# Later blocks' layer normalisation one slot later and behind VectorE's earlier work; V's split two slots behind its squares

## The chip, the cores and the metric

The kernel runs on one core of a Trainium2 chip. TensorE (PE) multiplies matrices, VectorE (DVE), ScalarE (ACT) and GpSimd (POOL) do the elementwise work, and SyncE (SP) mostly issues transfers. Each engine has an order of its own, fixed when the kernel is built; between engines, semaphores hold an instruction until its data are there. The metric is the device time of one execution, in microseconds; lower is better.

## The reference

Three parts run one behind the other on a batch of 4 sequences of 576 rows of 512: block-causal attention with 8 heads, a feed-forward network with layer normalisation and a residual, and a second one in front of which the rows are mixed by a two-dimensional Fourier transform.

```
# attention: q, k, v (4, 8, 576, 64), mask by blocks of 64
scores = scale * np.matmul(q, k.transpose(0, 1, 3, 2))
scores = np.where(mask, scores, -1000000000.0)
attn = np.exp(scores - np.max(scores, axis=-1, keepdims=True))
attn = attn / (np.sum(attn, axis=-1, keepdims=True) + 1e-09)
x = np.matmul(attn, v)                    # then heads side by side: (4, 576, 512)
# first feed-forward network
xn = (x - mu) / np.sqrt(var + 1e-06) * g_ln
x = x + np.maximum(xn @ w_ch1, 0.0) @ w_ch2       # 512 -> 2048 -> 512
# mixing and second feed-forward network
u = x + np.real(np.fft.fft(np.fft.fft(x, axis=1), axis=2))
un = (u - mu) / np.sqrt(var + 1e-06)
return u + np.maximum(un @ w_ch1_2, 0.0) @ w_ch2_2
```

## The kernel before

Every float32 operand of a large product is split into two fp16 parts (high and low), and three products of the parts take the place of one.

**Tiles.** The 2304 rows lie in nine blocks of 256, two half blocks of 128 each (`t` = 0, 1): E0 to E3 and F0 to F3, two for each sequence, and L, which collects 32 + 32 rows of each sequence. Attention works in units of a sequence and a pair of heads; each unit has three steps `j` = 2, 3, 4, which produce N, and when the last unit of a sequence is through, `a_x` moves N by GpSimd's DMA queue into XxF and XxL. E blocks are ready early, so the first network runs in the order E0 E1 E2 E3 F0 F1 L F2 F3 beside the attention of later sequences.

**One block of the first network.** `ln` computes mean and variance (bn_stats, bn_aggr) and, in twelve small operations (L532 to L547), one over the root. For each half block `ln_hi` normalises (xn, L564) and takes the high part (xs, ScalarE L571), `ln_lo` the low part (xs, VectorE L594) and issues a transposing transfer to xnT on SP (L595). There is one buffer each of xn, xs and xnT. Then come eight groups of products with the first weights (G1, `gemm1`, L627), each with two operations that make hT (L636, L637), and the products with the second weights (G2, `gemm2`, L652), half block by half block; the result is added to the rows of X (L664).

**Attention.** Scores (L1143, L1152), their maximum (aq, L1163, L1164), exponential (L1167), fp16 parts P (L918, L919), transposing transfers to PT on SP (L925), products with V (pv, L890), the division by the row sum (rr, L932, L935) and N (L1212, L1218). V is split into vh and vl: `a_norm` takes its squares, `a_total` sums them over partitions on GpSimd, `a_split` makes a power of two from it (pw, four operations, L835 to L842) and the two parts (L1127, L1128).

**Second weights.** From some 430 us on the second network's weights are decoded: a load wr (L202), a sign (ScalarE L217), ws (VectorE L218), squares (junk, L239), their sum (wn, wt), a scale (wsc, again four operations from L835 on), wq (L331, L339) and a spill to memory d (L348). The mixing of the rows (pq, ya, y) begins behind it.

**What sets the order.** Each part is a stream of items with a due time. `merge` takes the stream whose time is least, but not before the items that it needs are there (`have`), and so writes one program. A scheduler then orders each engine's instructions; within limits it moves one forward if its operands are there by its own estimate. `tc.issue_after(i)` is an edge that keeps what is written under it behind instruction `i`. In attention's stream `at(t, rank, f, u)` puts step `f` of unit `u` into slot `t`; a slot is 4.0 long, `f = 3 * n` is the slot in which unit `n` starts, P_N = 4, P_D = 0. `gives` says which slot makes a block's rows available to the first network.

Of the kernel before, what the change touches and what calls it, by code (L numbers as in the profile page):

```python
# [8 lines left out]
F32 = mybir.dt.float32  # L9
# [8 lines left out]
B, H, S, D = 4, 8, 576, 64  # L18
# [25 lines left out]
P_D = 0  # L44
# [34 lines left out]
P_N = 4  # L79
P_R = 0.5  # L80
# [19 lines left out]
def fused_kernel(ctx: ExitStack, tc: tile.TileContext, io: dict):  # L100
    nc = tc.nc
# [5 lines left out]
    sm = ctx.enter_context(tc.tile_pool(name="sm", bufs=2))  # L107
# [415 lines left out]
    def ln(ffn, c):  # L523
        x = X[c]
        w = sm.tile([128, 20], F32, tag="ln", bufs=2, name=f"ln{ffn}{c}")
        mv = w[:, 0:4].rearrange("p (t k) -> p t k", t=2)
        for t in range(2):
            st = sm.tile([128, 6], F32, tag="bn", bufs=2, name=f"bn{ffn}{c}{t}")
            nc.vector.bn_stats(out=st, in_=x[:, t, :])
            nc.vector.bn_aggr(out=mv[:, t, :], in_=st)  # L530
        v, e, y, a, y2 = (w[:, i:i + 2] for i in (4, 6, 8, 10, 12))
        nc.vector.tensor_scalar(  # L532
            out=v, in0=mv[:, :, 1], scalar1=1e-6, scalar2=None, op0=ALU.add
        )
        nc.vector.tensor_scalar(
            out=e.bitcast(I32), in0=v.bitcast(I32), scalar1=-1, scalar2=1,
            op0=ALU.bitwise_xor, op1=ALU.logical_shift_right,
        )
        nc.vector.tensor_scalar(
            out=y, in0=e, scalar1=float(0.677 * 2.0 ** -65), scalar2=None, op0=ALU.mult  # L540
        )
        for it in range(3):
            nc.vector.scalar_tensor_tensor(
                out=a, in0=y, scalar=-0.5, in1=y, op0=ALU.mult, op1=ALU.mult
            )
            nc.vector.tensor_tensor(out=a, in0=a, in1=v, op=ALU.mult)
            nc.vector.scalar_tensor_tensor(  # L547
                out=y2, in0=a, scalar=1.5, in1=y, op0=ALU.add, op1=ALU.mult
            )
            y, y2 = y2, y  # L550
        if (ffn, c) == (1, ("E", 0)):
            xnT[ffn, c] = a_tile([128, 2, 4, 256], F16, "xnT0", "xnT0")
        else:
            xnT[ffn, c] = fpool.tile([128, 2, 4, 256], F16, tag="xnT", bufs=1, name=f"xnT{ffn}{c}")
        lnst[ffn, c] = (mv, y)

    def ln_hi(ffn, c, t):
        mv, y = lnst[ffn, c]
        own = (ffn, c) in TURN
        if own:  # L560
            xn = a_tile([128, DM], F32, "xn0", "xn0")
        else:
            xn = fpool.tile([128, DM], F32, tag="xn", bufs=1, name="xn")
        nc.vector.tensor_scalar(  # L564
            out=xn, in0=X[c][:, t, :], scalar1=mv[:, t, 0:1], scalar2=y[:, t:t + 1],
            op0=ALU.subtract, op1=ALU.mult,
        )
        if own:
            return ln_turn(ffn, c, t, xn)
        xs = fpool.tile([128, 2, DM], F16, tag="xs", bufs=1, name="xs")  # L570
        nc.scalar.activation(out=xs[:, 0, :], in_=xn, func=AF.Copy)  # L571
        lnst[ffn, c, t] = (xn, xs)
# [16 lines left out]
    def ln_lo(ffn, c, t):  # L589
        if (ffn, c) in TURN:  # L590
            return
        xn, xs = lnst.pop((ffn, c, t))
        eng = nc.gpsimd if (ffn, t) in LNP else nc.vector
        eng.tensor_tensor(out=xs[:, 1, :], in0=xn, in1=xs[:, 0, :], op=ALU.subtract)  # L594
        nc.sync.dma_start_transpose(  # L595
            out=xnT[ffn, c].rearrange("p a k t -> p (a k) t")[:, :, t * 128:(t + 1) * 128],
            in_=xs.rearrange("p a f -> p (a f)"),
        )

    def ln_steps(ffn, c):  # L600
        return [
            (0.0, lambda: ln(ffn, c)), (0.0, lambda: ln_hi(ffn, c, 0)),
            (0.0, lambda: (ln_lo(ffn, c, 0), ln_hi(ffn, c, 1))), (0.0, lambda: ln_lo(ffn, c, 1)),
        ]

    def run(steps):
        for _, f in steps:
            f()
# [212 lines left out]
    def a_tile(shape, dt, tag, name):  # L821
        return ap_["p"].tile(shape, dt, tag=tag, bufs=ap_["b"][tag], name=name)
# [418 lines left out]
    def attention_items(order):  # L1241
        units = [(u, j) for u in order for j in (2, 3, 4)]
        ev = {}

        def at(t, rank, fn, *a):
            ev.setdefault(t, []).append((rank, len(ev.get(t, [])), fn, a))

        for n, u in enumerate(order):
            f = 3 * n
            at(max(f - 3 - L_N, f - 6), 9, a_load, u)  # L1250
            at(f - P_N, P_R, a_norm, u)
            at(f - P_N + P_D, P_R, a_total, u)
            at(f - P_N + P_D, P_R, a_split, u)
        lag = (0,) + LG
        gives = {}
        for t, (u, j) in enumerate(units):
            at(t, RK[0], a_s, u, j)
            at(t + lag[1], RK[1], a_exp, u, j)
            at(t + lag[2], RK[2], a_norm_p, u, j)
            at(t + lag[3], RK[3], a_pv, u, j)  # L1260
            at(t + lag[4], RK[4], a_evac, u, j)
            if j == 4 and u[1] == NPAIR - 1:
                at(t + lag[5], RK[5], a_x, u[0])
                gives[t + lag[5]] = ("X1", ("F", u[0]))

        def emit(t):
            for rank, n, fn, a in sorted(ev.get(t, []), key=lambda x: x[:2]):
                if fn is a_s and "f" in ff_last:
                    with tc.issue_after(ff_last["f"]):
                        fn(*a)  # L1270
                else:
                    fn(*a)

        return [
            (4.0, lambda t=t: emit(t), (), gives.get(t)) for t in range(min(ev), max(ev) + 1)
        ]
# [251 lines left out]
    if True:  # L1528
# [41 lines left out]
        AE = [e_items(b) for b in range(B)]  # L1570
        A1 = [(0.0, a_switch, (("W", 1, 2, 3), ("X1", ("E", 3))), None)]
        A1 += attention_items([(b, p) for b in range(B) for p in range(NPAIR)])
        A1 += [(0.0, a_end, (), ("X1", "L"))]

        LN = []

        def ffn_items(ffn, order, both=(), mixed=None):
            seq = []
            for n, c in enumerate(order):
                x = ("X", ffn, c) if ffn == 2 else ("X1", c)  # L1580
                behind = ((("G1",) + TURN[0] + (5,)),) if (ffn, c) == TURN[1] else ()
                lns = [(0.0, f, (x,) + behind, None) for _, f in ln_steps(ffn, c)]
                g1_needs = ()
                if ffn == 1 and n < LNA:
# [195 lines left out]
```

## Time and profile before

| | us |
|---|---|
| three runs | 994.78, 996.1, 999.83; median 996.1 |
| profiled execution | 997.26 |
| its span | 995.5 |
| busy in the span: TensorE | 946.1 (95%) |
| VectorE | 673.7 (68%) |
| ScalarE | 490.2 (49%) |
| GpSimd | 72.5 (7%) |

The span is the time from the first to the last instruction in the trace; 1.8 us of the profiled execution lie around it. All times of the trace count from the start of the span. A wait is put down to the instruction that released it last: "pv <- DVE aq" says that TensorE's product pv could start when VectorE's aq was through, and that may be late because of something else in front of it on VectorE.

### The profile page before, as it was taken

To read this page: it belongs to the slowest core of one execution; us is meant where nothing else is said; L and a number is where in the kernel's file an instruction comes from. 1 tells how busy PE (TensorE), PEld (TensorE's weight loads), DVE (VectorE), ACT (ScalarE), POOL (GpSimd) and SP (SyncE) were. 2 spreads that over 40 slices of the span, in tenths; PEclk is the share of its full clock that TensorE was granted. 3 is DMA by queue.
4 is the path that set the end of the run, shared out by engine and by line. 5 is a ranking of instruction groups with operands and counts; after the bars stand their busy time and mean duration, and the time that the engine had idled before them with its cause. 6 is when DMAs were issued, how large, how long until landed. Compare 5 with 4: busy or idle time off the path is not lost.

```text
span 995.5 us, 19447 instructions
## 1 busy us (share of the span) xinstructions
PE 946.1 (95%) x7758; PEld 700.8 (70%) x7758; DVE 673.7 (68%) x1677; ACT 490.2 (49%) x852; POOL 72.5 (7%) x184
## 2 busy tenths in 40 slices
PE   8898989998998999998999889999999999999998
PEld 6786654674674674766576665858588888888887
DVE  3886696665767666566587887669476776765754
ACT  5887664554554564426656654325153352342431
POOL 1000000002001010040011120100000000000000
PEclk9998999999999999999999989999999999999999
DMA  7657536758667666567408657011110111101100
GB/s 259 225 186 212 133 79 138 153 114 154 139 126 154 129 146 103 99 139 298 146 8 249 212 177 255 8 22 65 43 22 23 33 23 33 22 23 43 23 22 22
DMA packets 159195, 110.95 MB, mean 111 GB/s; under 512 B 134141, under 2 KB 141318, under 8 KB 157056
## 3 DMA queue, kind: packets, MB, share of 16 engines
q1 hardware_dynamic: 154640, 104.87, 40.8%
q0 software_dynamic: 2352, 4.32, 1.9%
q8 instruction: 61, 1.00, 0.4%
q10 hardware_dynamic: 2112, 0.52, 0.2%
q14 instruction: 30, 0.25, 0.1%
HBM read 64.19 MB, written 11.01 MB: 76 GB/s over the span
## 4 chain that ended last, share of the span: by engine, by line
PE 42%; DVE 7%; DMA 5%; ACT 3%; issue 1%; POOL 0%; ACTq 0%; POOLq 0%; DVEq 0%; SPq 0%
PE g L698 15%; PE s L748 13%; PE g L627 6%; PE g L679 4%; PE g L652 3%; DMA wr<-in_w 2%; DMA xnT1L<-xs 1%; ACT junk L239 1%; DVE ws L218 1%; DVE wq L339 1%; ACT sign L217 1%; DVE hT L637 1%; PE ya L1433 1%; DMA xnT2('F', 0)_7977<-xs 1%; DMA d<-ws 1%
## 5 line engine op out<-in xcount | busy, mean ns | idle before, releaser
L627 PEld LDWEIGHTS <-wq 128*128 128x128 f16 x2112 | 206.5, 99 | 47.9 <-issue 19.0
L652 PE MATMUL g<-wq,hT 128*128 128x512 f16 x768 | 184.2, 383 | 2.1 <-ACT hT L636 1.3
L698 PEld LDWEIGHTS <-wq 128*128 128x128 f16 x1344 | 131.5, 98 | 15.4
L652 PEld LDWEIGHTS <-hT 128*128 128x128 f16 x768 | 74.6, 99 | 90.2 <-issue 5.8
L748 PEld LDWEIGHTS <-hs 128*128 128x128 f16 x1176 | 115.1, 98 | 13.3
L715 ACT ACTIVATE hr<-g,tk 128x256 f32<-128x256 f32 x112 | 47.0, 470 | 143.1 <-PE g L698 143.1
L890 PE MATMUL pv<-vh,PT 128*128 128x65 f16 (+1 forms) x704 | 102.9, 203 | 14.6 <-DMA PT<-P 5.3
L919 DVE SCALAR_TENSOR_TENSOR P<-e,P 128x768 f16<-128x768 f32 (+2 forms) x56 | 54.6, 976 | 69.9 <-ACT P L918 69.8
L890 PEld LDWEIGHTS <-PT 128*128 128x128 f16 x1056 | 82.1, 101 | 28.1 <-issue 19.0
L723 DVE TENSOR_TENSOR hr<-hr 128x128 f32<-128x128 f32 x224 | 65.4, 292 | 48.3 <-ACT hr L715 40.4
L1167 ACT ACTIVATE e<-st,aq 128x384 f32<-128x384 f32 (+2 forms) x80 | 48.9, 652 | 91.3 <-DVE aq L1164 80.8
L748 PE MATMUL s<-tT,hs 128*128 128x256 f16 x672 | 75.7, 273 | 0.0
L637 DVE SCALAR_TENSOR_TENSOR hT<-g,hT 128x512 f16<-128x512 f32 x88 | 59.8, 683 | 19.3 <-ACT hT L636 19.1
L636 ACT ACTIVATE hT<-g 128x512 f16<-128x512 f32 x88 | 51.4, 588 | 34.2 <-PE g L627 34.1
L679 PE MATMUL g<-wq,hT 128*128 128x512 f16 x288 | 63.8, 379 | 0.2 <-DVE wq L339 0.2
L890 PE MATMUL pv<-vl,PT 128*128 128x64 f16 (+1 forms) x352 | 62.7, 203 | 0.0
L730 DVE TENSOR_TENSOR hs<-hr,hs 128x896 f16<-128x896 f32 x56 | 60.8, 1085 | 0.5
L748 PE MATMUL s<-tB,hs 128*128 128x256 f16 x504 | 57.3, 273 | 0.0
L218 DVE SCALAR_TENSOR_TENSOR ws<-wr,sign 128x512 int32<-128x512 int32 (+1 forms) x48 | 41.2, 863 | 23.2 <-ACT sign L217 20.6
L217 ACT ACTIVATE sign<-wr 128x512 f16<-128x512 bf16 (+1 forms) x48 | 46.5, 971 | 19.7 <-DMA wr<-in_w 19.0
L729 ACT ACTIVATE hs<-hr 128x896 f16<-128x896 f32 x56 | 53.1, 948 | 1.6 <-DVE hr L723 1.6
L679 PEld LDWEIGHTS <-hT 128*128 128x128 f16 x288 | 28.0, 98 | 32.4 <-issue 0.5
(425 smaller groups left out, 1516.4 us busy)
## 6 DMA issues: line engine op xcount, KB each, us to landing
wr<-in_w SPq DMA_DIRECT2D x16, 1023.5 KB, 6.0
wr<-in_w SPq DMA_DIRECT2D x32, 511.8 KB, 5.1
rawv<-in_vt SPq DMA_DIRECT2D x16, 320.0 KB, 2.9
k<-in_kt SPq DMA_DIRECT2D x16, 288.0 KB, 3.5
d<-ws SPq DMA_DIRECT2D x4, 1024.0 KB, 5.2
ws<-d SPq DMA_DIRECT2D x4, 1024.0 KB, 5.5
wt<-d SPq DMA_DIRECT2D x4, 1024.0 KB, 4.8
qz<-in_qt SPq DMA_DIRECT2D x32, 80.0 KB, 3.2
```

The source lines that it names most:

```text
L217: nc.scalar.activation(out=z[:, :, :, 1], in_=r.bitcast(BF16)[:, :, :, 2], func=AF.Copy)
L627: nc.tensor.matmul(out=ps[:, i, :], lhsT=w1(ffn, k, wh, m), rhs=xt[:, xh, k, :], start=(n == 0), stop=(n == 3 * KT - 1),)
L637: nc.vector.scalar_tensor_tensor(out=h[:, :, 1, :], in0=ps, scalar=0.0, in1=h[:, :, 0, :], op0=ALU.max, op1=ALU.subtract,)
L652: nc.tensor.matmul(out=ps, lhsT=h[f // 4][:, f % 4, hh, t * 128:(t + 1) * 128], rhs=w2(ffn, f, wh), start=(f == 0 and hh == 0 and wh == 0) ...
L679: nc.tensor.matmul(out=g2["b"][t], lhsT=h[f // 4][:, f % 4, hh, t * 128:(t + 1) * 128], rhs=w2(ffn, f, wh), start=(f == 0 and hh == 0 and ...
L698: nc.tensor.matmul(out=ps[:, q, :], lhsT=w1(2, k, wh, i + 8 * q), rhs=xt[:, xh, k, :], start=(n == 0), stop=(n == 3 * KT - 1),)
L723: done = nc.vector.tensor_tensor(out=r[:, o], in0=r[:, a], in1=r[:, b], op=op)
L729: nc.scalar.activation(out=h[:, 0], in_=r[:, 1:8], func=AF.Copy)
L730: nc.vector.tensor_tensor(out=h[:, 1], in0=r[:, 1:8], in1=h[:, 0], op=ALU.subtract)
L748: nc.tensor.matmul(out=ps, lhsT=h[:, hh, hb], rhs=T[nm][:, wh, i], start=(i == 0 and hh == 0 and wh == 0), stop=(i == 7 and hh == 1),)
L890: nc.tensor.matmul(out=out[..., 0:w], lhsT=l, rhs=v[..., 0:w], start=(n == 0), stop=(n == len(mm) - 1))
L919: nc.vector.scalar_tensor_tensor(out=P[:, 1, 0:n], in0=e, scalar=PSC, in1=P[:, 0, 0:n], op0=ALU.mult, op1=ALU.subtract)
```

## The change

There are three edits. In `ln`, for the blocks F0 to F3 and L of the first network, the statistics get an edge: they stay behind the last VectorE instruction that was written until then (`last_on`, new). In `attention_items`, `a_split` goes into slot f - 2; it was in f - 4, with `a_norm` and `a_total`. And the rows of F0, F1 and F2 (not those of the last sequence, F3) are given to the first network one slot later.

```diff
--- before.py
+++ after.py
@@ -524,10 +524,13 @@
         x = X[c]
         w = sm.tile([128, 20], F32, tag="ln", bufs=2, name=f"ln{ffn}{c}")
         mv = w[:, 0:4].rearrange("p (t k) -> p t k", t=2)
-        for t in range(2):
-            st = sm.tile([128, 6], F32, tag="bn", bufs=2, name=f"bn{ffn}{c}{t}")
-            nc.vector.bn_stats(out=st, in_=x[:, t, :])
-            nc.vector.bn_aggr(out=mv[:, t, :], in_=st)
+        with ExitStack() as order:
+            if ffn == 1 and c[0] != "E":
+                order.enter_context(tc.issue_after(last_on(mybir.EngineType.DVE)))
+            for t in range(2):
+                st = sm.tile([128, 6], F32, tag="bn", bufs=2, name=f"bn{ffn}{c}{t}")
+                nc.vector.bn_stats(out=st, in_=x[:, t, :])
+                nc.vector.bn_aggr(out=mv[:, t, :], in_=st)
         v, e, y, a, y2 = (w[:, i:i + 2] for i in (4, 6, 8, 10, 12))
         nc.vector.tensor_scalar(
             out=v, in0=mv[:, :, 1], scalar1=1e-6, scalar2=None, op0=ALU.add
@@ -602,6 +605,9 @@
             (0.0, lambda: ln(ffn, c)), (0.0, lambda: ln_hi(ffn, c, 0)),
             (0.0, lambda: (ln_lo(ffn, c, 0), ln_hi(ffn, c, 1))), (0.0, lambda: ln_lo(ffn, c, 1)),
         ]
+
+    def last_on(engine):
+        return next(i for i in reversed(nc.cur_bb.bb.instructions) if i.engine == engine)
 
     def run(steps):
         for _, f in steps:
@@ -1250,7 +1256,7 @@
             at(max(f - 3 - L_N, f - 6), 9, a_load, u)
             at(f - P_N, P_R, a_norm, u)
             at(f - P_N + P_D, P_R, a_total, u)
-            at(f - P_N + P_D, P_R, a_split, u)
+            at(f - P_N + 2, P_R, a_split, u)
         lag = (0,) + LG
         gives = {}
         for t, (u, j) in enumerate(units):
@@ -1261,7 +1267,7 @@
             at(t + lag[4], RK[4], a_evac, u, j)
             if j == 4 and u[1] == NPAIR - 1:
                 at(t + lag[5], RK[5], a_x, u[0])
-                gives[t + lag[5]] = ("X1", ("F", u[0]))
+                gives[t + lag[5] + (0 if u[0] == B - 1 else 1)] = ("X1", ("F", u[0]))
 
         def emit(t):
             for rank, n, fn, a in sorted(ev.get(t, []), key=lambda x: x[:2]):
```

The following pieces show what that does to the order of the engines. Line numbers of the changed kernel are 3 to 6 higher (L529 is L532, L594 is L597, L664 is L670, L919 is L925).

VectorE at F0's statistics, before: they stand in front of attention's P, maximum aq and N of a unit, behind nothing but the maximum (L1163, L1164) of the step before.

```order
L1164 TENSOR_SCALAR aq<-aq 128x2
L529 BN_STATS bn1('F', 0)0_3913<-XxF_2949 128x6
L529 BN_STATS bn1('F', 0)1_3916<-XxF_2949 128x6
L664 SCALAR_TENSOR_TENSOR XxE_1058<-g_2690,winv_1540,XxE_1058 128x512
L919 SCALAR_TENSOR_TENSOR P<-e,P 128x768
L1163 TENSOR_REDUCE aq<-st 128x2
L932 TENSOR_SCALAR rr<-pv,pw 128x2
L1164 TENSOR_SCALAR aq<-aq 128x2
L530 BN_AGGR ln1('F', 0)_3912<-bn1('F', 0)0_3913 128x2
L935 RECIPROCAL rr<-rr 128x2
L530 BN_AGGR ln1('F', 0)_3912<-bn1('F', 0)1_3916 128x2
```

The changed kernel, the same engine, some hundred rows later in its order, behind the first half of E3's output (XxE_1444):

```order
L670 SCALAR_TENSOR_TENSOR XxE_1444<-g_3656,winv_1540,XxE_1444 128x512
L925 SCALAR_TENSOR_TENSOR P<-e,P 128x1024
L938 TENSOR_SCALAR rr<-pv,pw 128x2
L1169 TENSOR_REDUCE aq<-st 128x1
L941 RECIPROCAL rr<-rr 128x2
L1170 TENSOR_SCALAR aq<-aq 128x1
L532 BN_STATS bn1('F', 0)0_3906<-XxF_2942 128x6
L1218 TENSOR_TENSOR N_3832<-pv,rr 128x128
L533 BN_AGGR ln1('F', 0)_3905<-bn1('F', 0)0_3906 128x2
L532 BN_STATS bn1('F', 0)1_3909<-XxF_2942 128x6
L925 SCALAR_TENSOR_TENSOR P<-e,P 128x576
```

F0's statistics moved behind attention's work of about three units, into the gaps between single rows of it.

VectorE at L's statistics, before: they stand between the hT of F1's G1 (L637) and the last N of attention, and F2's first statistics are among them.

```order
L637 SCALAR_TENSOR_TENSOR hT<-g_5213,hT 128x2x256
L637 SCALAR_TENSOR_TENSOR hT<-g_5270,hT 128x2x256
L529 BN_STATS bn1L_5543<-XxL 128x6
L530 BN_AGGR ln1L<-bn1L_5543 128x2
L529 BN_STATS bn1L_5546<-XxL 128x6
L529 BN_STATS bn1('F', 2)0_6040<-XxF_4756 128x6
L530 BN_AGGR ln1L<-bn1L_5546 128x2
L637 SCALAR_TENSOR_TENSOR hT<-g_5297,hT 128x2x256
L932 TENSOR_SCALAR rr<-pv,pw 128x2
```

The changed kernel: the hT of F1 come first, then ws, the second network's weights (L218), then the first half of F1's output (L670), then L's statistics.

```order
L643 SCALAR_TENSOR_TENSOR hT<-g_5402,hT 128x2x256
L218 SCALAR_TENSOR_TENSOR ws_5806<-wr_5804,sign_5490 128x512
L218 SCALAR_TENSOR_TENSOR ws_5806<-wr_5839,sign_5491 128x512
L218 SCALAR_TENSOR_TENSOR ws_5806<-wr_5845,sign_5490 128x512
L218 SCALAR_TENSOR_TENSOR ws_5806<-wr_5864,sign_5491 128x512
L670 SCALAR_TENSOR_TENSOR XxF_3846<-g_5429,winv_1540,XxF_3846 128x512
L532 BN_STATS bn1L_5543<-XxL 128x6
L532 BN_STATS bn1L_5546<-XxL 128x6
L533 BN_AGGR ln1L<-bn1L_5543 128x2
L250 TENSOR_REDUCE wn_5870<-wn 128x1
L533 BN_AGGR ln1L<-bn1L_5546 128x2
```

L's statistics moved behind four ws and XxF; F2's and F3's, which stood right behind them, went further back still.

SP's queue at L's transposes, before: the first stands behind attention's last PT, two weight loads lie between the two.

```order
L925 DMA_TRANSPOSE PT<-P 128x16x128
L925 DMA_TRANSPOSE PT<-P 128x10x128
L595 DMA_TRANSPOSE xnT1L<-xs 128x8x128
L202 DMA wr_5804<-in_w_2 128x2047
L202 DMA wr_5839<-in_w_2 128x2047
L595 DMA_TRANSPOSE xnT1L<-xs 128x8x128
L202 DMA wr_5845<-in_w_2 128x2047
L202 DMA wr_5864<-in_w_2 128x2047
L202 DMA wr_5875<-in_w_2 128x2047
```

The changed kernel: eight weight loads stand further up, and these rows follow.

```order
L202 DMA wr_5917<-in_w_2 128x2047
L202 DMA wr_5935<-in_w_2 128x2047
L202 DMA wr_5946<-in_w_2 128x2047
L202 DMA wr_5969<-in_w_2 128x2047
L348 DMA d_5897<-wq_5874 128x4096
L598 DMA_TRANSPOSE xnT1L<-xs 128x8x128
L202 DMA wr_5988<-in_w_2 128x2047
L202 DMA wr_5994<-in_w_2 128x2047
L598 DMA_TRANSPOSE xnT1L<-xs 128x8x128
```

L's transposes moved behind ten weight loads and the first spill (L348).

VectorE at F3's splits, before: both low parts (L594) stand in front of L's output (XxL, L664) of the first network.

```order
L218 SCALAR_TENSOR_TENSOR ws_6020<-wr_6234,sign_5491 128x512
L637 SCALAR_TENSOR_TENSOR hT<-g_5812,hT 128x2x256
L594 TENSOR_TENSOR xs<-xn,xs 128x512
L564 TENSOR_SCALAR xn<-XxF_5442,ln1('F', 3)_6702 128x512
L594 TENSOR_TENSOR xs<-xn,xs 128x512
L564 TENSOR_SCALAR xn<-XxF_5442,ln1('F', 3)_6702 128x512
L664 SCALAR_TENSOR_TENSOR XxL<-g_5851,winv_1540,XxL 128x512
L664 SCALAR_TENSOR_TENSOR XxL<-g_6005,winv_1540,XxL 128x512
```

The changed kernel, at F3's second low part (L597): the second half of F2's output (XxF_4749, L670) stands in front of it.

```order
L549 TENSOR_TENSOR ln2('F', 0)_7958<-ln2('F', 0)_7958 128x2
L550 SCALAR_TENSOR_TENSOR ln2('F', 0)_7958<-ln2('F', 0)_7958 128x2
L218 SCALAR_TENSOR_TENSOR ws_6764<-wr_7007,sign_5491 128x512
L670 SCALAR_TENSOR_TENSOR XxF_4749<-g_6689,winv_1540,XxF_4749 128x512
L597 TENSOR_TENSOR xs<-xn,xs 128x512
L250 TENSOR_REDUCE wn_7013<-wn 128x1
L1398 TENSOR_TENSOR xe<-XxE_1058,XxF_4749 128x1024
L841 TENSOR_SCALAR pw<-wt 128x1
```

F3's second split moved from in front of L's output to behind the end of F2's.

## Rows read from the trace of the kernel before

**Rows 1.** The page's table of busy time: engine, us busy, share of the span, instructions.
```profile
PE 946.1 (95%) x7758; PEld 700.8 (70%) x7758; DVE 673.7 (68%) x1677; ACT 490.2 (49%) x852; POOL 72.5 (7%) x184
```

**Rows 2.** Waits of TensorE, 170 to 560 us: engine, line, waited for: us, times, longest.
```profile
PE pv L890 <- DVE aq L1164: 4.0, 1, 4.0
PE g L627 <- DVE pw L842: 3.8, 2, 2.1
PE g L627 <- DVE hT L637: 3.5, 3, 2.0
PE g L627 <- DMA wr<-in_w: 2.6, 1, 2.6
PE pv L890 <- DVE N L1212: 2.5, 3, 1.6
PE pv L890 <- DVE ln1('F', 0)_3912 L532: 2.5, 1, 2.5
PE pv L890 <- DMA PT<-P: 1.5, 1, 1.5
```

**Rows 3.** Timeline of VectorE at F0: start, us, operation, xcount [idle before <-releaser].
```profile
244.72 0.69 DVE L529 BATCH_NORM_STATS2 bn1('F', 0)0_3913<-XxF 128x6 f32<-128x512 f32 x1 [4.51 <-DMA XxF<-N]
...
249.24 0.16 DVE L532 TENSOR_SCALAR ln1('F', 0)_3912<-ln1('F', 0)_3912 128x2 f32<-128x2 f32 x1
```

**Rows 4.** Windows behind two pauses: busy us by engine, then PEclk, DMA share, GB/s.
```profile
250.00:254.00 4.00, 4.00 (x19) 2.03 (x18) 3.72 (x14) 1.28 (x2) 0.20 (x1) 0.57 0.54 131
318.00:322.00 4.00, 4.00 (x20) 1.99 (x18) 3.17 (x8) 2.44 (x4) 0.00 (x0) 0.57 0.01 4
```

**Rows 5.** Timeline of VectorE at F1.
```profile
314.90 0.55 DVE L564 TENSOR_SCALAR xn<-XxF,ln1('F', 1)_4868 128x512 f32<-128x512 f32 x1
...
317.28 0.28 DVE L1212 TENSOR_TENSOR N<-pv,rr 128x128 f32<-128x128 f32 x1
```

**Rows 6.** Instructions on L's transposed rows xnT1L, waits, and time from issue to landing.
```profile
L627 PE MATMUL g<-xnT1L,wq x192: 269/273/421, 456.1 to 480.8; 128*128 128x256 f16 x192
...
  DVE hT L637: 2.0, 1
...
  ACT xs L571: 8.9, 1
...
DMA to landing us min/median/max: 3.1/7.9/12.6
```

**Rows 7.** Timeline of VectorE before L's matmuls.
```profile
451.26 0.69 DVE L594 TENSOR_TENSOR xs<-xn,xs 128x512 f16<-128x512 f32 x1 [8.88 <-ACT xs L571]
...
454.68 0.69 DVE L218 SCALAR_TENSOR_TENSOR ws<-wr,sign 128x512 int32<-128x512 int32 x1 [1.45 <-ACT sign L217]
455.29 0.74 DVE L664 SCALAR_TENSOR_TENSOR XxF<-g,winv,XxF 128x512 f32<-128x512 f32 x1
```

**Rows 8.** Lines L652 (425 to 460) and L627 (545 to 600): ns min/median/max, first and last start.
```profile
L652 PE MATMUL g<-wq,hT x96: 376/379/379, 432.6 to 453.1; 128*128 128x512 f16 x96
...
L627 PE MATMUL g<-xnT1('F', 3)_6721,wq x192: 270/273/421, 553.5 to 592.9; 128*128 128x256 f16 x192
```

**Rows 9.** Groups of VectorE by line, 425 to 560 us: busy us, mean ns.
```profile
L339 DVE SCALAR_TENSOR_TENSOR wq<-ws,wsc,wq 128x512 f16<-128x512 f32 x16 | 11.0, 744 | 1.8 <-ACT wq L331 1.8
```

**Rows 10.** Chain of waits, 540 to 600 us: start, us, what.
```profile
555.95 0.80 ACT sign L217
...
557.49 0.72 ACT junk L239 x2
...
577.75 1.25 PE pq L1467 x5
```

**Rows 11.** Waits of TensorE, 540 to 600 us.
```profile
PE pq L1467 <- ACT y L1440: 5.2, 2, 4.7
PE ya L1433 <- DVE y L1441: 1.9, 1, 1.9
```

**Rows 12.** Timeline of SP's queue at the spills.
```profile
559.64 0.33 SPq L348 DMA_DIRECT2D d<-ws  x1
```

## The prediction

> **What bounds the kernel now.** I read the page first: TensorE is busy 95% of the span, so an order of work can win time only where it stands still or runs at the low clock [rows 1]. Then the waits of TensorE in the stretch where the change acts (170 to 560 us, attention and the first feed-forward network): the seven longest entries make 20.4 us, 16.3 of them put down to VectorE [rows 2]. That is all a better order of VectorE could win there, plus the slow clock behind each pause. Last I read VectorE's timeline at those pauses, the windows of the clock, and the stretch around 577 us, where TensorE waits for the chain that decodes the second network's weights and prepares the mixing [rows 10, 11]. From 577.75 us on the chain of waits is TensorE alone [rows 10], so a gain or loss before it counts only if it gets past that point.
>
> The profiled execution took 997.26 us, 1.1 us above the median of the runs; the sum is made against it.
>
> **Attention stretch, normalisation of F0 and F1.** Before, F0's statistics are hoisted so far up that VectorE, which works in order, has nothing else from 240.2 us on and stands 4.51 us for the transfer of F0's rows, and the chain's small operations (0.16 us each) lie in front of attention's P and N [rows 3]. TensorE pays 2.5 us right behind it (the wait named L532) and, just before, 1.5 us for a PT that comes from a late P [rows 2]. F1's chain has its first normalisation at 314.90, the N behind it comes at 317.28, and TensorE stands 4.0 us for the aq behind that [rows 2, 5]. Now both chains stand some hundred rows of VectorE's order later (F0) and behind what was given (F1), mixed singly with attention's rows, and their transfers have landed. Gross: 2.5 + 1.5 + 4.0 = 8.0. Behind each of the two long pauses stands a stretch of 4 us at a granted clock of 0.57, that is mostly at the level of 1.2 GHz [rows 4]: 4 x 0.43 = 1.7 us each, 3.4 in all. Together 11.4 us.
>
> Against it: the same operations remain (four statistics of 0.69, two chains of twelve at 0.16, and per half block a normalisation of 0.55 and a split of 0.69 us [rows 3, 5, 7]) and still stand in front of some P or N. No row shows them there; bounds: nothing, or the pauses they made before, 11.4. I take the nearest rows, the three short waits for N (2.5 us together [rows 2]) and half as much again for the clock, about 4.0. Term: -7.4, between -11.4 and 0. The transposes of F0 and F1 land later but, by the order, still in front of the matmuls that read them; cover lost would cost one landing, 3.1 us [rows 6].
>
> **V's scale and split.** Two slots later in the stream, but VectorE's rows are the same up to F0, pw and vl included: the scheduler put them there anyway. The two waits for pw (3.8 us together [rows 2]) stay. Term 0; if slots further on do move, between -3.8 and +3.8.
>
> **The last block (L).** Before, its statistics were hoisted into attention's tail, its first transposes landed in 3.1 us, the second in 12.6, and its matmuls started at 456.1 [rows 6]. Now its statistics stand behind four ws and behind XxF's first half. The fourth ws was at 454.68 [rows 7]. It can come earlier, since before VectorE stood 8.88 us for ScalarE, which in its turn waited 8.9 us for the landing of 12.6 [rows 6, 7]; that wait is no longer in front of it. So the fourth ws lies between 445.8 and 454.7. From its start: ws 0.69, XxF 0.74, two statistics 1.38, two aggregates and twelve small ones 2.3, with four wq of 0.74 (3.0) [rows 9], six small operations on the weights' scale (1.0) and one normalisation (0.55) between: 9.6 us. ScalarE's first split 0.63, then four pairs of junk and sign in front of its second split, 4 x (0.72 + 0.80) = 6.1 [rows 10], 0.63, VectorE's 0.69, the landing 3.1: 11.2. L's matmuls so begin between 466.6 and 475.5, 10.5 to 19.4 us later; there is no other work for TensorE, whose last product of F1's G2 starts at 453.1 and lasts 0.4 [rows 8]. Ten weight loads and a spill stand in front of the first transposes now, so I do not take the early end but 468: +12. The wait of 2.0 us for hT inside L's matmuls [rows 6] goes, since ScalarE and VectorE are through with more of the decode by then: +10. The low clock behind the new pause I set at 1.7 us against as much that no longer follows the wait for hT: 0; no row shows what a pause of 12 us costs there.
>
> **F3.** Before, its splits were done with no wait for them. Now its second split stands on VectorE behind the second half of F2's output, which ends with G2 of F2. TensorE has nothing else then: 0.74 + 0.69 + 3.1 = 4.5, with issue some 4.7 us of pause, follows TensorE wherever it is. Upper bound: ScalarE's split waits behind a sign that was at 555.95 and the transposes behind the spill that was issued at 559.64 [rows 10, 12]; 559.64 + 0.33 + 3.1 = 563.1 against a start of 553.5 [rows 8], +9.6. F2's normalisation is late too, but still in front of its matmuls by the order: 0.
>
> **Sum.** TensorE reaches the mixing at -7.4 + 10 + 4.7 = +7.3. There it waited 1.9 + 5.2 = 7.1 us for y [rows 11]. If y keeps its time, these waits take up 7.1, and +0.2 is left. I let y keep it: VectorE wins up to 8.9 us of standing before and gets F3's 6.3 us of normalisation (1.38 + 2.3 + 1.1 + 1.4) into the stretch. 997.26 + 0.2 = 997.5; against the median of the runs, 1.1 lower, 996.4. I say 997.
>
> **Rivals.**
> *Slower: the transposes queue behind the weight loads.* L's second transposes took 12.6 us to land when loads were in flight, the first 3.1 [rows 6]. If both of L's, and F3's, land in 12.6, L's matmuls begin 9.5 us later than taken and F3's pause is 14.2 instead of 4.7: TensorE reaches the mixing at -7.4 + 19.5 + 14.2 = +26.3 at worst, past the 7.1 by 19; with only L's or only F3's, by about 10. I price it at 1007. It decides from the point where L's and F3's delays exceed 14.5 us together (7.4 + 7.1). For it: ten loads and two spills stand around these transposes now. Against: the wide landings of before fell on a stretch that also loads the mixing's constants. The rule behind it: the Trainium skill ("DMA: Bandwidth & Descriptors", Queues, rings and completion order) says that each DMA engine takes descriptors in ring order, and that SP owns one ring on each of them, so its loads and transposes share it; by it a transpose behind two loads waits for them, which favours this rival. The trace agrees for the second transposes of L, not for the first.
> *Faster: y comes earlier too.* If the decode, freed of the 8.88 us, carries y forward and L's delay is at its low end (+10.5 - 2 = +8.5), TensorE is at -7.4 + 8.5 + 4.7 = +5.8 and the pause of 7.1 is not all needed; with attention's term at its end (-11.4) it is at +1.8, and y up to 6 us earlier ends the time at 991; with y no limit at all, 990. For it: attention's waits are plain in the trace. Against: L and F3.
> *Nothing moves.* Were the waits put down to VectorE's chains really others', attention's term would be 0, and so would a good deal of the rest, 997. The order does change, so this is small.
>
> **How the numbers follow.** Forecast (losses in the tail take up the gain, 992 to 1003) 0.42; slower rival 0.30; faster rival 0.22; nothing moves 0.06. About 0.5%, 5 us, is what a measurement of this kernel can tell from no change: 991 to 1001. Faster: the rival's 0.22 and 0.04 of the forecast's low side, 0.26. Slower: 0.30 and 0.06 of its high side, 0.36. Same: 0.38. The range, 986 to 1010, takes in the ends of the rivals but for some 0.1 on each side.
>
> **What would show it.** Right: no wait of 4.0 and 2.45 us for VectorE between 240 and 320 us; the waits for pw still there; a pause of 10 to 16 us in front of L's matmuls; one of 5 to 10 in front of F3's; the wait for y before the mixing's pq gone or short. Wrong: L's matmuls within 5 us of the end of G2 of F1 (then faster), or F3's without a pause; or attention's small waits as large as before; or y later by as much as TensorE (then slower by the tail's whole loss).

## The result and the profile after

The changed kernel took 1011.57 us (median of 4 runs, 1006.56 to 1015.24), beside 996.96 us before (994.78 to 999.83): a ratio of 1.0137, with an interval of 1.0102 to 1.0173, slower by some 14 us. Two of the four runs after took about 1015 us, the profiled one among them, the other two 1006.6 and 1008.1. The profiled execution took 1015.06 us; its span is 1013.3 us, against 995.5.

Where the time went is seen by the first product of each block's G1 (from the start times of the products on each transposed tile xnT):

| first product of | before | after | later by |
|---|---|---|---|
| E2 | 187.5 | 191.3 | 3.8 |
| E3 | 262.5 | 265.7 | 3.2 |
| F0 | 335.1 | 338.7 | 3.6 |
| F1 | 403.8 | 411.7 | 7.9 |
| L | 456.1 | 472.1 | 16.0 |
| F2 | 503.4 | 515.1 | 11.7 |
| F3 | 553.5 | 578.9 | 25.4 |
| E0, second network | 622.0 | 639.8 | 17.8 |
| end of the span | 995.5 | 1013.3 | 17.8 |

The first 3.8 us are no part of the change: they are there at E2's first product, before VectorE's order differs at all (from F0's statistics at 244.7 us on), and the other traces of this study reach E2 at 184.5 to 188.8 us (last section). Counted from E2's first product the changed kernel loses 14.0 us, near the 14.6 between the medians. They come in three places: 4.7 us up to the last of F1's products (440.9 - 191.3 beside 432.4 - 187.5), 3.2 from there to F2's first, 13.7 from there to F3's first; 7.6 us are given back between F3 and the second network. E3 is no fair start for this count, since the pauses of 1.5 and 2.5 us of [rows 2] stand in front of it, at 242.7 and 249.5 us.

The waits of TensorE after (engine, line, waited for: us, times, longest), from 170 to 620 us:

```profile
PE g L633 <- DMA xnT1('F', 3)_6721<-xs: 13.6, 1, 13.6
PE g L633 <- DMA xnT1L<-xs: 10.1, 1, 10.1
PE pv L896 <- DVE rr L941: 4.8, 1, 4.8
PE pv L896 <- ACT N L1224: 4.6, 1, 4.6
PE pv L896 <- DMA PT<-P: 2.9, 1, 2.9
PE g L633 <- DVE pw L848: 2.1, 1, 2.1
PE g L633 <- DMA xnT1('F', 1)_4887<-xs: 1.8, 1, 1.8
```

Of the entries of [rows 2] the one for F0's chain (L532) and the 4.0 us for aq are gone (1.0 us for aq stands elsewhere, at 234 us); wr and, but for 0.2 us, hT are gone too, one of the two waits for pw is left, and the one for PT stands where it stood, 2.9 us where it was 1.5. In their place stand rr (4.8, just before F0's products) and N (4.6, just before F1's), and F1's products wait 1.8 us more for their rows. The waits for y of [rows 11] are gone. The two largest are the pauses before L's and F3's products, 10.1 and 13.6 us.

L, on VectorE (start, us, operation, [idle before <- releaser]):

```profile
446.48 0.69 DVE L218 SCALAR_TENSOR_TENSOR ws<-wr,sign 128x512 int32<-128x512 int32 x1 [3.92 <-ACT sign L217]
...
452.45 0.69 DVE L218 SCALAR_TENSOR_TENSOR ws<-wr,sign 128x512 int32<-128x512 int32 x1 [1.57 <-ACT sign L217]
453.06 0.74 DVE L670 SCALAR_TENSOR_TENSOR XxF<-g,winv,XxF 128x512 f32<-128x512 f32 x1
...
461.11 0.55 DVE L567 TENSOR_SCALAR xn<-XxL,ln1L 128x512 f32<-128x512 f32 x1
...
465.61 0.74 DVE L670 SCALAR_TENSOR_TENSOR XxF<-g,winv,XxF 128x512 f32<-128x512 f32 x1
...
468.11 0.69 DVE L597 TENSOR_TENSOR xs<-xn,xs 128x512 f16<-128x512 f32 x1
```

The rows are the first and the fourth ws, XxF's first half, L's first xn, XxF's second half, L's second xs. Before [rows 7], XxF's first half was at 455.29 and L's transposes had long been issued. Now everything of L follows that row, and 15 us pass from it to the second xs. From the fourth ws to the end of the first xn it is 9.2 us, and 10.4 from there to L's first product; the prediction had worked out 9.6 and 11.2. The transposes themselves are quick, both landing in some 3.1 us where one of [rows 6] took 12.6:

```profile
L633 PE MATMUL g<-xnT1L,wq x192: 272/273/422, 472.1 to 494.3; 128*128 128x256 f16 x192
...
DMA to landing us min/median/max: 3.1/3.1/3.2
```

F3, on VectorE: the first statistics, the first xn, F2's second half, and the second xs, then TensorE's wait:

```profile
553.44 0.68 DVE L532 BATCH_NORM_STATS2 bn1('F', 3)0_6703<-XxF 128x6 f32<-128x512 f32 x1
...
566.81 0.53 DVE L567 TENSOR_SCALAR xn<-XxF,ln1('F', 3)_6702 128x512 f32<-128x512 f32 x1
...
573.35 0.74 DVE L670 SCALAR_TENSOR_TENSOR XxF<-g,winv,XxF 128x512 f32<-128x512 f32 x1
574.01 0.68 DVE L597 TENSOR_TENSOR xs<-xn,xs 128x512 f16<-128x512 f32 x1
```

```profile
578.95 5.28 PE L633 MATMUL g<-xnT1('F', 3)_6721,wq 128*128 128x256 f16 x24 [13.63 <-DMA xnT1('F', 3)_6721<-xs]
```

From statistics to xn it is 13.4 us. In [rows 8] F3's products began at 553.5, when now the statistics have only begun. The chain's own operations take some 4 us of that; the others are the mixing's preparation, the weights' decode and the second network's normalisation, all on VectorE. F2's second half stands behind such rows too: it is added at 573.35, 8.0 us after the end of TensorE's last product of F2 (578.95 - 13.63 = 565.3).

The clock behind the two pauses (busy us by engine, PEclk, DMA share, GB/s):

```profile
472.00:476.00 4.00, 3.94 (x24) 3.02 (x25) 2.43 (x4) 3.47 (x9) 0.00 (x0) 0.64 0.91 260
579.00:583.00 4.00, 4.00 (x20) 2.75 (x20) 1.99 (x5) 3.48 (x7) 0.00 (x0) 0.50 0.62 237
```

0.64 and 0.50 over 4 us, beside 0.57 in [rows 4]: four or five times the pause of 2.5 us, and about the same time at the low level (0.50 is 1.2 GHz).

### The profile page after: what moved, and what is told of

It is laid out like the page before. It is cut to its first block, busy times and chain, and to the rows that moved or that the text cites. A ratio compares the mean times of both kernels' runs of the same rounds, so it can differ in the third digit from the quotient of the medians.

```text
span 1013.3 us, 19432 instructions
## 1 busy us (share of the span) xinstructions
PE 952.0 (94%) x7758; PEld 705.6 (70%) x7758; DVE 674.5 (67%) x1677; ACT 490.6 (48%) x852; POOL 72.1 (7%) x184
## 4 chain that ended last, share of the span: by engine, by line
PE 54%; DMA 6%; DVE 5%; ACT 2%; issue 1%; POOL 0%; SPq 0%; ACTq 0%; POOLq 0%; DVEq 0%
PE g L704 14%; PE s L754 13%; PE g L633 12%; PE g L658 6%; PE g L685 4%; DMA wr<-in_w 2%; DMA d<-ws 1%; PE ya L1439 1%; PE pv L896 1%; PE st L1149 1%; DMA xnT1('F', 0)_3924<-xs 1%; DMA xnT1('F', 1)_4887<-xs 1%; DVE ws L218 1%; DMA xnT2('F', 0)_7977<-xs 1%; PE st L1158 1%
## 5 line engine op out<-in xcount | busy, mean ns | idle before, releaser
L896 PE MATMUL pv<-vh,PT 128*128 128x65 f16 (+1 forms) x704 | 99.4, 204 | 17.3 <-DMA PT<-P 6.3
L925 DVE SCALAR_TENSOR_TENSOR P<-e,P 128x768 f16<-128x768 f32 (+2 forms) x56 | 54.7, 977 | 76.0 <-ACT P L924 75.7
L896 PEld LDWEIGHTS <-PT 128*128 128x128 f16 x1056 | 79.3, 101 | 28.6 <-issue 18.6
L896 PE MATMUL pv<-vl,PT 128*128 128x64 f16 (+1 forms) x352 | 60.4, 204 | 0.0
L218 DVE SCALAR_TENSOR_TENSOR ws<-wr,sign 128x512 int32<-128x512 int32 (+1 forms) x48 | 41.4, 866 | 25.0 <-ACT sign L217 22.0
```

The lines of the kernel that those rows point to most:

```text
L218: nc.vector.scalar_tensor_tensor(out=W["st", ffn, which, c][:, i:i + n, :].bitcast(I32), in0=r.bitcast(I32)[:, :, :, 0], scalar=13, in1=z. ...
L896: nc.tensor.matmul(out=out[..., 0:w], lhsT=l, rhs=v[..., 0:w], start=(n == 0), stop=(n == len(mm) - 1))
L925: nc.vector.scalar_tensor_tensor(out=P[:, 1, 0:n], in0=e, scalar=PSC, in1=P[:, 0, 0:n], op0=ALU.mult, op1=ALU.subtract)
```

## The experiments

Ratios are to the kernel before, timed on the same chip, five rounds each.

**The edits apart.** Four kernels: V's split alone, and the edge alone for F0 and F1, for L, for F3. The condition in `ln` was the only difference between the last three:

```diff
-            if ffn == 1 and c[0] != "E":
+            if ffn == 1 and c in (("F", 0), ("F", 1)):     # or ("L",), or (("F", 3),)
```

> The kernel before with the second edit alone: V's split two slots later. By the order, some forty rows of VectorE round F1's normalisation change places, nothing else. Theory A (the loss of 15 us comes from the edge in front of the statistics, through F0 and F1, L and F3): no change, 994 to 1000 us, the waits for pw (2.1 and 1.7 us) still there. Rival B (attention is slower because V's split is late): a pause for pw or vl of over 3 us in attention and 1000 us or more.

> The kernel before with the edge for the statistics of F0 and F1 alone. Theory A: the pauses of 2.5 and 4.0 us go, but two others come, since both half blocks are now split close together and the second has to wait, with one buffer xs, until the first transposes have landed (3.1 us), with attention's rr behind it on VectorE: pauses of some 4.8 us before F0's matmuls and 4.6 + 1.8 us before F1's, L's matmuls 3 to 6 us later than 456.1; the waits before the mixing (7.1 us) take this up, so the total is 995 to 1001 us. Rival C (the attention part of the prediction was right, and the run with the trace only disturbed): L's matmuls at 449 to 452, total 990 to 996.

> The kernel before with the edge for L's statistics alone. Theory A: a pause of 8 to 13 us before L's matmuls, made by VectorE's and ScalarE's order and not by the transposes, which land in 3.1 us; the waits of 2.0 and 1.3 us behind it go and the 7.1 us before the mixing take most of the rest: 996 to 1002 us. Rival D (each delay reaches the end in full): 1003 to 1007 us.

> The kernel before with the edge for F3's statistics alone. Theory A: F3's chain stands on VectorE among the mixing's preparation and the second network's normalisation; a pause of 10 to 16 us before F3's matmuls (553.5 before), 6 to 8 of it taken back by the waits before the mixing: 1001 to 1006 us, more than from any other of the edges alone. Rival E (F3's pause is mostly behind L's lateness, 4.7 us of it its own): 996 to 999 us.

| kernel | median us | ratio | interval |
|---|---|---|---|
| V's split alone | 997.38 | 0.9998 | 0.9977 to 1.0020 |
| edge for F0 and F1 | 999.74 | 1.0014 | 0.9994 to 1.0035 |
| edge for L | 1005.84 | 1.0081 | 1.0049 to 1.0112 |
| edge for F3 | 1000.63 | 1.0029 | 1.0006 to 1.0051 |

The parts add up to 1.0122, within the interval of the whole. The split does nothing that can be measured. The slot of `gives` wasn't run: with it alone, the order of every engine is that of the kernel before. F2's edge wasn't run by itself. L is the largest part, where rival D held and theory A fell; F3's is smaller than theory A said.

With the edge for F0 and F1 alone, ScalarE (P, then the second xs), SP and TensorE round F0:

```profile
323.59 1.06 ACT L924 ACTIVATE P<-e 128x1024 f16<-128x1024 f32 x1
326.80 0.63 ACT L574 ACTIVATE xs<-xn 128x512 f16<-128x512 f32 x1 [2.16 <-DMA xnT1('F', 0)_3931<-xs]
```

```profile
319.56 1.29 SPq L931 DMA_TRANSPOSE PT<-P  x1
320.90 8.52 SPq L598 DMA_TRANSPOSE xnT1('F', 0)_3931<-xs  x2
329.54 1.83 SPq L931 DMA_TRANSPOSE PT<-P  x1
```

```profile
330.28 0.22 PE L896 MATMUL pv<-vh,PT 128*128 128x65 f16 x1 [6.33 <-DVE rr L938]
```

The second split (326.80) stands 2.16 us for the landing of the first transposes, 5.9 us after their issue, since there is one buffer xs. SP's row of 320.90 holds both transposes, the second behind the first's landing; the transposes of attention's P, issued at 329.54, stand behind them on SP, and ScalarE's and VectorE's next rows behind the split. TensorE pays 6.33 us. Counted from E2's first product, the last of F1's comes 2.9 us later than before.

The wait for the buffer is not new. Before, ScalarE's second splits of F0 and F1 stood longer for it:

```profile
302.29 0.63 ACT L571 ACTIVATE xs<-xn 128x512 f16<-128x512 f32 x1 [1.97 <-DMA xnT1('F', 0)_3931<-xs]
...
378.00 0.63 ACT L571 ACTIVATE xs<-xn 128x512 f16<-128x512 f32 x1 [3.30 <-DMA xnT1('F', 1)_4887<-xs]
```

That is 5.3 us in all, where the changed kernel has 0.50 and 1.89. New is what waits behind it: before, TensorE had no pause behind the first and 1.6 us for N some 5 us behind the second.

With the edge for L alone, TensorE's waits from 440 to 640 us:

```profile
PE g L633 <- DMA xnT1L<-xs: 15.2, 1, 15.2
PE pq L1473 <- ACT y L1446: 4.3, 2, 3.8
PE ya L1439 <- DVE y L1447: 3.1, 1, 3.1
```

Counted from E2's first product (186.5 us here), L's products began 12.2 us later than before, F2's 8.0 later, and the second network's 8.7 later. The waits for y are 7.4 us in all, where [rows 11] show 7.1. They took up nothing. With the edge for F3 alone the waits for y are gone, and this is the whole list from 540 to 640 us:

```profile
PE g L633 <- DMA xnT1('F', 3)_6721<-xs: 13.1, 1, 13.1
```

F3's products began 12.6 us later there, counted in the same way, and the second network's 5.0 later.

**Delay alone.** Does lateness of TensorE at L reach the end, and at F3? The kernel before with idle products in `gemm1`:

```diff
         ps = g_tile([128, 2, 256], "g1")
+        if ffn == 1 and mp == 0 and c == "L":          # or ("F", 3)
+            busy(64, ps[:, 0, :])
```

> The kernel before with 64 idle products of 256 columns on TensorE in front of L's first products, some 7 us that change nothing else; the order of some twenty rows round them shifts. Theory G (y, for which the mixing waits, hangs on L's output through VectorE and ScalarE, so lateness of TensorE at L reaches the end in full): the waits for y stay at 5 to 8 us, total 1003 to 1006 us. Rival H (as predicted, y keeps its time, and its 7 us of waiting take the delay up): waits for y under 2 us, total 996 to 999 us.

> The kernel before with the same 64 idle products in front of F3's first products. Theory G: from here on VectorE, ScalarE and the loads run on towards y while TensorE is late, so that the waits for y take up most: total 996 to 1000 us. If lateness at F3 too reaches the end in full: 1003 to 1006 us.

At L: 1005.27 us, 1.0079 (1.0049 to 1.0109). At F3: 999.56 us, 1.0031 (1.0009 to 1.0054). The waits from 540 us on, with the delay at L:

```profile
PE pq L1475 <- ACT y L1448: 5.2, 2, 4.7
PE ya L1441 <- DVE y L1449: 1.9, 1, 1.9
```

These are the entries of [rows 11] to the tenth: theory G at L, and H is refuted. Counted from E2's first product, L's first came 5.7 us later and the end of the span 7.0. With the delay at F3 pq's wait is gone and ya's is larger:

```profile
PE ya L1441 <- DVE y L1449: 4.7, 1, 4.7
```

There 7.1 us at F3's first product became 3.5 at the second network's (557.0 and 621.9, against a trace that is 3.6 us early at F2's).

**The changed kernel without one of its edges.**

> The changed kernel without the edge for L's statistics, all else as changed. If the losses add up (L's edge alone 8 us, F3's 3, F0's and F1's 1.5): 1001 to 1005 us, L's matmuls within 4 us of the end of F1's. If L's loss is shared with the others (F3's pause is longer when L is early): 1006 to 1010 us.

> The changed kernel without the edge for F3's statistics. If F3's part is what its edge alone showed, 3 us less than the changed kernel: 1007 to 1010 us, the pause of 13.6 us gone and waits for y of 6 to 8 us back in its place. If F3's pause is additive: 1001 to 1004 us.

Without L's: 999.92 us, 1.0033 (1.0011 to 1.0055), less than both expectations. Without F3's: 1005.58 us, 1.0094 (1.0068 to 1.0119), between the two. In its trace pq's wait of 5.2 us is back. L's edge costs 10 to 12 us inside the change, F3's 4 to 6, by the differences of the ratios and of the medians; each is uncertain by some 4 us. That only 3.2 us stand between F1's last product and F2's first in the changed kernel does not speak against it: counted from E2's first product, F2's first is 7.9 us late with L's edge and 0.3 us early without it, although F1's last is 2.4 us late there too.

**F0 and F1 with a second buffer, and earlier.** The second half block of F0 and F1 gets a buffer of its own in attention's pool:

```diff
-        xs = fpool.tile([128, 2, DM], F16, tag="xs", bufs=1, name="xs")
+        if ffn == 1 and c in (("F", 0), ("F", 1)) and t == 1:
+            xs = a_tile([128, 2, DM], F16, "xsb", "xsb")
+        else:
+            xs = fpool.tile([128, 2, DM], F16, tag="xs", bufs=1, name="xs")
```

> The kernel before with the edge for F0 and F1, as in the run with that edge alone, and a second buffer for the split of their second half block (xsb). Theory A (with one buffer the second split, its transposes and, behind them on SP, ScalarE and VectorE in order, attention's next PT and rr wait until the first transposes have landed): the pauses of 6.3 and 4.8 us before F0's and F1's matmuls fall under 2.5 us each, L's matmuls begin 4 to 9 us earlier than with one buffer, total 989 to 996 us. Rival F (the pauses come from the load of VectorE's operations themselves, xn, xs and the chain, in front of attention's): they stay at 4 to 6 us, total 997 to 1002 us.

996.41 us, 1.0000 (0.9980 to 1.0020). Neither expectation held. The waits for rr and N are gone, but these came at the same two places:

```profile
PE g L636 <- DMA xnT1('F', 1)_4887<-xsb: 4.6, 1, 4.6
PE g L636 <- DMA xnT1('F', 0)_3931<-xsb: 4.3, 1, 4.3
```

The products of F0 and F1 now wait for their own transposes: the chain is late as such. What the buffer does by itself isn't separated, since VectorE's order changes with it: the second low part now stands in front of attention's P, and stood behind it. So the four steps of the normalisation were written earlier among the quarters of G2 (`prev`), from the first quarter on (s = 0) or the third (s = 2), where they stood at the fifth to eighth:

```diff
+                if ffn == 1 and order[n] in (("F", 0), ("F", 1)):
+                    for i in range(len(prev)):
+                        out += prev[i:i + 1] + (lns[i - s:i - s + 1] if i >= s else [])
```

> The edge for F0 and F1 alone and the second buffer, and the four steps of their normalisation given to the program two quarters of a half block of G2 (some 5 us) earlier. Theory A: with two buffers the pauses of 4.3 and 4.6 us were the transposes themselves, asked for too late; earlier by 5 us, they go, the old pauses of 2.5, 1.5 and 4.0 us do not come back, L's matmuls begin 4 to 8 us earlier and, since lateness at L reaches the end in full, so does the time: 988 to 993 us. Rival I (attention's load on VectorE makes up the pauses elsewhere, or L waits for its own normalisation): 994 to 999 us.

> As the last one with one buffer. Theory A: the second split waits for the first transposes again, with attention's work behind it: pauses of 3 to 6 us in front of pv, 994 to 1000 us, above the run with two buffers by 2 to 6 us. If one buffer is enough when the steps come earlier: the same as with two.

> As the run with two buffers, the steps a whole half block of G2 (some 10 us) earlier. Theory A: no better than 5 us earlier, 988 to 994 us; if VectorE now waits for the rows of F0 or F1 again, a pause in attention and 994 to 999 us.

| edge for F0, F1 and | median us | ratio | interval |
|---|---|---|---|
| two buffers, s = 2 | 992.32 | 0.9945 | 0.9921 to 0.9969 |
| one buffer, s = 2 | 993.88 | 0.9976 | 0.9959 to 0.9993 |
| two buffers, s = 0 | 989.85 | 0.9936 | 0.9911 to 0.9961 |

Faster than before. With one buffer the long waits for rr and N are gone as well, and this is left of N from 230 to 450 us:

```profile
PE pv L896 <- DVE N L1218: 5.1, 4, 3.4
```

Its 993.88 us lie just under what was expected of one buffer, and its interval overlaps that of two, so what the second buffer adds isn't shown. With two buffers and s = 2 a wait for aq of 3.8 us is there. For s = 0 the largest waits of TensorE from 300 to 450 us, where 4.0, 4.8 and 6.3 had stood, are:

```profile
PE pv L899 <- DVE N L1221: 2.4, 2, 1.6
PE g L636 <- DVE XxF L673: 2.2, 1, 2.2
PE g L636 <- DVE pw L851: 2.1, 1, 2.1
```

Is it the edge, or the rest?

> The kernel before with the second buffer for F0's and F1's second half block alone, no edge, no step moved. Theory A: before, the halves are far apart and wait for no buffer, so nothing is gained: 994 to 999 us, the pauses of 2.5 and 4.0 us still there. Rival J (the second buffer is what made the faster version faster): 988 to 993 us.

> The faster version (two buffers, steps a half block of G2 earlier) without the edge. Theory A: without the edge the scheduler hoists F0's and F1's statistics to where VectorE stands for their rows again: 994 to 999 us, pauses of 2.5 to 4 us back. Rival K (the earlier steps do it, the edge is of no use): 988 to 993 us.

The buffer alone: 994.63 us, 0.9985 (0.9965 to 1.0005). Buffer and earlier steps (s = 0) without the edge: 996.12 us, 0.9994 (0.9976 to 1.0011). J and K are refuted: for F0 and F1 it takes the edge, with the steps early enough for what follows.

**L earlier.** The edge for L alone, with its steps from the first quarter on (the same code, for "L").

> The edge for L alone, with L's four normalisation steps given to the program a half block of G2 (some 10 us) earlier, so that its statistics stand in front of the first ws. Theory A (L's loss is the place, behind the decode's first group): the pause before L's matmuls falls from 15.2 to under 8 us, total 996 to 1000 us. Rival: the loads and spills round the transposes keep it at 10 us or more, total 1002 to 1007 us.

993.26 us, 0.9973 (0.9959 to 0.9986): better than expected. The pause of 15.2 us fell to

```profile
PE g L633 <- DMA xnT1L<-xs: 2.7, 1, 2.7
```

L's earlier steps without the edge weren't run, so the edge's part in this gain isn't shown.

**Both.**

> The faster version (edge, second buffer and steps a half block of G2 earlier for F0 and F1) and the edge with the earlier steps for L. If the gains add up (6.4 and 2.7 us): 985 to 989 us. If the waits before the mixing's first ya limit both: 988 to 992 us.

985.42 us, 0.9898 (0.9872 to 0.9924), 11 us faster than before and 26 faster than the changed kernel: the gains (0.64% and 0.27%) add up. Its largest waits after 170 us, beside the two for pw:

```profile
PE pv L899 <- DVE N L1221: 4.2, 4, 1.6
...
PE ya L1442 <- issue: 3.9, 1, 3.9
PE g L636 <- DMA xnT1L<-xs: 2.8, 1, 2.8
```

## Why the prediction was wrong

It forecast 997 us, no change; 1011.57 lies above its range. Its slower rival's 1007 is nearer, but that rival's way, transposes behind loads, is not what happened. The prediction's sum beside the trace, counted from E2's first product:

| term | forecast | measured |
|---|---|---|
| F0 and F1, up to F1's last product | -7.4 | +4.7 |
| L, from there to F2's first product | +10 | +3.2 |
| F3, from there to its first product | +4.7 | +13.7 |
| taken up by the waits for y | -7.1 | -7.6 |
| sum | +0.2 | +14.0 |

With the 3.8 us at E2 this makes the 17.8 of the span. Two terms failed, the price of F0's and F1's chains at their new place, and F3's pause.

- **V's split, 0:** right, 0.9998.
- **F0 and F1, -7.4 us:** the removal was right for the 2.5 and the 4.0 us; the 1.5 us for PT, at 242.7 us, lie in front of F0's statistics (244.7 [rows 3]) and were not theirs. The price of what came was wrong. "I take the nearest rows, the three short waits for N" is the step that failed: a pause of 4.8 and one of 4.6 + 1.8 us came. From E2's first product to F1's last it takes 249.6 us after (440.9 - 191.3) and took 244.9 before: +4.7, outside the bounds of -11.4 to 0. The upper bound took the old pauses as the worst. What it left out is the chain's way to its own products: the prediction names it ("cover lost would cost one landing, 3.1 us") and puts it at nothing, and with a second buffer that is what TensorE stood for, 4.3 and 4.6 us. That the two transposes of one block stand next to each other with one buffer was to be seen in the order too; before, they were 8 us apart, and ScalarE waited for the buffer even so.
- **L, +12 at its first product, +10 in all:** the pause (10.1; 15.2 alone) is in the forecast's 10 to 16. By its own edge the first product came 12.2 us later, and 8.0 us of that were left at F2. The 3.2 us of the table are less because F0's and F1's lateness and L's don't add up there. The mechanism, VectorE's and ScalarE's order behind the decode, is shown by the run with earlier steps.
- **F3, +4.7:** this step failed as well. The pause is 13.6 us, 13.1 alone, above the upper bound of 9.6. The working priced only what follows F2's second half, which it set right behind the end of F2's G2. That half came 8.0 us behind it, and 5.6 us more passed to F3's first product. It left out that the whole chain, which before lay at 434 to 540 us, now runs among the mixing's work on VectorE.
- **"I let y keep it":** by the number this came out, 7.6 us of 21.6, since F3's pause alone uses the waits for y up. As a mechanism it was wrong for L. The idle products at L moved the end by 0.79% with the waits for y unchanged, and without F3's edge the waits are back and L's lateness reaches the end (1.0094). For lateness at F3 it held in part: 7.1 us became 3.5. The chain of waits of the kernel before leads from L's last products through XxL to the mixing's preparation (start, us, what):

```profile
492.16 11.41 PE g L652 x52
503.59 0.76 DVE XxL L664
504.38 0.69 DVE xe L1368
```

I took what is tied to TensorE for a resource with a time of its own. That XxL is the tie, rather than the hT in front on VectorE, wasn't tried.
- **Rivals.** *Transposes behind loads:* wrong. Ten loads and a spill stand ahead on SP, and yet both of L's transposes landed in 3.1 us, and F3's in 4.2 and 4.5. The loads had been issued by 453.5, ten us earlier; the spill, issued at 461.2, landed in 4.0 us, 1.4 us before the first transposes. So the rule on the order within a ring, which the Trainium skill ("DMA: Bandwidth & Descriptors", Queues, rings and completion order) gives, was neither broken nor of any price here: what stood ahead was nearly through. It does not explain the 12.6 us of [rows 6] either, as the prediction read it: the two loads ahead had landed at 439.9 us, 2.0 us after those transposes were issued. The other 10.6 us pass while six later loads and, on GpSimd's queue, the mixing's constants are in flight, issued from 435.9 to 439.9 us, the last of them landing at 450.9 (KB each, us from issue to landing):

```profile
c_ct<-in_c_ct POOLq DMA_DIRECT2D x1, 289.0 KB, 6.3
...
c_sd<-in_c_sd POOLq DMA_DIRECT2D x1, 255.0 KB, 11.9
```

In the changed kernel these constants have landed by 457.0 us, before L's transposes are issued at 463.5. This is what the prediction held against the rival, that the wide landings of before fell on the stretch which loads the constants. That they were the cause isn't shown; no run moved them alone. *Faster:* attention lost time instead of gaining it; a gain there appeared only in kernels that mend the waits. *Nothing moves:* true of the second and third edits.
- **The signs named in advance:** the two waits between 240 and 320 us went, and the pause at L and the vanished wait for pq came, as described under "right"; F3's pause was longer than the 5 to 10 us named, and one of the two waits for pw went. Of "wrong", the small waits in attention came too, and larger.

## What to carry to other kernels

Where an edge moves a chain of steps later, price the chain's whole way to what reads it, transfers included: with a second buffer the products of F0 and F1 still stood 4.3 and 4.6 us for their own transposes. Here the edge paid only where the steps were also written earlier: by itself it cost 0.14% (within the noise) at F0 and F1 and 0.81% at L, with earlier steps the kernels were 0.64% and 0.27% faster than before. Where two of the steps share a buffer and stand close together, the second waits for the first's transfer, and every in-order queue behind it waits along; what that costs by itself is not separated here. Before a wait is counted as slack, follow what it waits for back to its start: if that is the engine whose lateness it is to take up, it takes up nothing (0.79% for some 7 us of idle products at L). And one rule for all blocks had a different price at each of them, so the edges are best tried one by one.

## What the runs showed of the hardware

The start differs from run to run. These are 40 to 60 us after and before, where every engine's order is the same:

```profile
40.00:60.00 20.00, 20.00 (x157) 17.84 (x158) 13.56 (x35) 16.25 (x26) 0.77 (x2) 0.88 0.51 182
```

```profile
40.00:60.00 20.00, 19.98 (x178) 17.68 (x178) 14.90 (x37) 18.69 (x29) 0.77 (x2) 1.00 0.60 207
```

With the same work the granted clock was 0.88 in one and 1.00 in the other. E2's first product came at 184.5 to 191.3 us over the traces of this study, so that spans of two traces are compared from a common block on, and not from zero.

The time at the low clock hardly grows with the pause of TensorE in front of it: windows of 2 us show 0.50 and 0.77, then full, behind 10.1 us at L; 0.50, 0.50 and 0.72, then full, behind 13.6 at F3; 0.57 and 0.57, then full, behind the 2.5 us of before. Each window's length times what is missing to 1.00 makes 1.5, 2.6 and 1.7 us. A short pause does not always bring it: the 2.1 us for pw in front of one of E2's products are followed by 0.50 and 0.67 in the trace before and by 1.00 after.
